# A new hand-written order of TensorE's 531 tasks in an attention and expert-attention kernel

## The chip, the cores and the metric

The kernel runs on one core of a Trainium2 chip. The metric is the time of one execution on the device in microseconds (us), as a median over runs: 588.84 us for the kernel before, over three runs from 587.78 to 590.09.

## What is computed

The inputs are q, k, v of 8 batches, 8 heads, 576 positions and 64 features in float32, a gate matrix and four experts' projections. A first attention with a mask by blocks of 64 runs on every head:

```python
scores = scale * np.matmul(q, k.transpose(0, 1, 3, 2))
mask = block_i >= block_j
attn = softmax(np.where(mask, scores, -1e9))
x = (attn @ v) as (batch, 576, 512)
```

Its output x goes into a mixture of four experts. Each is a causal attention of its own with 64 features (q = x @ wq[e], and so on), followed by a projection to 512. A gate (logits = x @ w_gate) picks two experts for each position, and their outputs are summed with softmax weights.

## The kernel before, in words

Five engines work from in-order queues: TensorE (PE) multiplies, VectorE (DVE) and ScalarE (ACT) do the masks, exponentials and copies, GpSimd (POOL) takes subtractions, SyncE (SP) issues transfers. The program is written out by a planner that runs while the kernel is built. Functions add tasks to `Plan` (line 407), each with an engine, a cost in ns, a key, the tasks that it depends on and the buffers that it takes and frees. `Plan.run` (line 442) then walks through time as the costs have it and gives each engine its next task.

For ACT, DVE, POOL and SP the next task is the one with the lowest key whose buffers are free; `at` (line 339) adds to a key what the table `MOVE` (line 57) holds under the task's name. For PE the order is given: `LINE` (line 311) lists all 531 PE tasks by their number in the order of adding, and PE takes them one by one (lines 456 and 457). PE's planned costs, among them `PRICE` (line 352) for going from one kind of task to another, only set the plan's clock, and so what the other engines choose.

The work is cut into 48 slots: 32 for the first attention (A, batch b, pair of heads p, written here A b.p) and 16 for the experts (M b.p, two pairs of experts for each batch). The PE tasks have four kinds (`mode`):

- S, scores (`f_s`, line 911): q and k in float32 or as a sum of high and low parts (`hl`, `lo`), 64 rows of the array for each head of the pair, so two products run side by side. A slot has three: the one of 448 columns (tiles 0 and 1, named :0), of 448 (tile 2, :2) and of 576 (tile 3, :3). The first slot has four.
- T, transposes (`f_t`, line 978): the exponentials e against a unit matrix, 64 rows each, three for each slot.
- C, attention times values (`f_av`, line 1102): eTa or eTb against va, vm or vz, 128 rows and 64 columns, two for each slot (:0 with eTa, 24 matmuls; :1 with eTb, 32).
- F, full array: projections to the experts' q and k (8 for each batch, 12 matmuls), to v (5), and the output (4 or 5 for each batch, 10 for the last).

Three ways to divide the array follow (`TILING`): S and T use halves of the rows, C halves of the columns, F the whole.

After an S task DVE masks the scores and finds each row's bound (`f_m`), ACT takes the exponentials and their sums (`f_e`), and T can run; DVE or ACT copy the transposes out of PSUM (`f_v`), and C can run. The sums go through ACT and DVE (`f_r1` to `f_rt`), then by a transfer to memory (dr<-rT) and by another back, spread over the partitions (rs<-dr). DVE multiplies the product of a C task with rs (`f_p1`, x<-bank,rs) and so frees its PSUM bank. There are eight banks; `MOST` (line 346) allows at most three of them to C tasks and projections ("m"), two to outputs ("o"), six to scores, six to transposes.

Of the kernel before, what the change touches and what calls it, by code (L numbers as in the profile page):

```python
# [20 lines left out]
P = 128  # L21
# [317 lines left out]
def at(key, b, *tag):  # L339
# [9 lines left out]
FEW = 4  # L349

TILING = {"F": "F", "C": "C", "S": "H", "T": "H"}
PRICE = {"FC": 120, "FS": 197, "FT": 100, "CF": 215, "CS": 182, "CT": 143, "SF": 214, "SC": 155, "ST": 20,
         "TF": 204, "TC": 125, "TS": 33}

STAY = 3.99
# [287 lines left out]
def attention_moe(ctx: ExitStack, tc, qk, v, w, wo, out):  # L643
# [13 lines left out]
    plan = Plan(pools, tc, log)  # L657
# [218 lines left out]
    def add_attention(si):  # L876
        kind, b, p = slots[si]
        causal = kind == "M"
        v_s = V[slots[si]]
        if kind == "A":  # L880
            obuf, odeps = loads[b, p]
            ops = lambda: raw[obuf.idx]
            hl = parts[b, p]
# [534 lines left out]
```

## Time and profile before

| what | value |
| --- | --- |
| median of 3 runs | 588.84 us (587.78 to 590.09) |
| the profiled execution, its own time | 585.91 us |
| span of its trace, first to last instruction | 584.0 us |
| mean granted clock of TensorE in it | 0.998 |

The profiled execution is 2.93 us, or 0.5%, under the median; 1.91 us of its time lie outside the span. Times in the rows below count from the start of the span. In the trace all of the program's instructions carry one line, so they are told apart by tiles: bank<-raw, bank<-hl,lo and their like are S, bank<-id,e is T, bank<-eTa,va (vm, vz) and bank<-eTb,va are C, bank<-x,wh, bank<-wh,x and bank<-woh,y are F.

### The profile page before, as it was taken

The numbers are of one execution on the slowest core, as the hardware profiler recorded it, in microseconds if no ns is written. First come the engines' busy times: TensorE is split into PE (matmuls) and PEld (weight loads), VectorE is DVE, ScalarE is ACT, GpSimd is POOL, SyncE is SP. The second block draws the span as 40 slices with busy tenths as digits, with TensorE's granted clock in tenths as the row PEclk, the third lists the DMA queues.
The fourth block names the chain that finished last, engine by engine and source line by source line (L and its number), as shares of the span: only waits on it lengthen the run. The fifth ranks groups of instructions, "written<-read, shape, count | busy, mean of one in ns | idle before, by whom it ended". The sixth has DMA issues, their size and how long they took to land.

```text
span 584.0 us, 19808 instructions
## 1 busy us (share of the span) xinstructions
PE 567.0 (97%) x7794; PEld 524.8 (90%) x7794; DVE 472.9 (81%) x1669; ACT 449.0 (77%) x1406; POOL 169.5 (29%) x248
## 2 busy tenths in 40 slices
PE   7889999999999999999999999999999999999996
PEld 5779999999999998999999999888999999999874
DVE  7888889799878789988988788898879869964751
ACT  6988789778877778877888688877688869865652
POOL 1275235233331233430425213432221323130101
PEclk9999999999999999999999999999999999999999
DMA  6657134422533225441354212452342403220032
GB/s 229 182 186 236 54 125 112 140 85 67 156 126 92 92 86 167 131 144 42 97 188 145 85 62 85 141 164 83 125 134 85 132 17 97 66 63 21 37 117 90
DMA packets 29852, 65.50 MB, mean 112 GB/s; under 512 B 9664, under 2 KB 10176, under 8 KB 29760
## 3 DMA queue, kind: packets, MB, share of 16 engines
q1 hardware_dynamic: 29616, 64.08, 34.8%
q8 instruction: 61, 1.00, 0.7%
q14 instruction: 31, 0.25, 0.1%
q10 hardware_dynamic: 144, 0.16, 0.1%
HBM read 54.01 MB, written 10.22 MB: 110 GB/s over the span
## 4 chain that ended last, share of the span: by engine, by line
PE 83%; DMA 6%; ACT 4%; DVE 4%; issue 1%; SPq 1%; POOL 0%; DVEq 0%; ACTq 0%
PE bank L389 83%; ACT e L389 2%; DVE bank L389 2%; DMA raw<-in_qk_dram 2%; DMA rs<-dr 2%; DMA out_dram<-ob 1%; DMA dr<-rT 1%; DVE x L389 1%; SPq L389 1%; ACT ob L389 0%; ACT eTb L389 0%; ACT el L389 0%; DVE eTa L389 0%; DVE nm L389 0%; ACT vz L389 0%
## 5 line engine op out<-in xcount | busy, mean ns | idle before, releaser
L389 ACT ACTIVATE e<-bank,nm 128x320 f32<-128x320 f32 (+3 forms) x384 | 218.9, 580 | 24.9 <-DVE nm L389 22.5
L389 DVE CUSTOM_DVE_ANT_0 bank<-bank,mask_a 64x64 f32<-64x64 f32 (+2 forms) x320 | 154.7, 503 | 13.8 <-PE bank L389 6.9
L389 PE MATMUL bank<-x,wh 128*128 128x256 f32 (+1 forms) x512 | 105.0, 299 | 0.0
L389 POOL TENSOR_TENSOR lo<-raw,hl 128x320 fp32r<-128x320 f32 x81 | 68.7, 876 | 114.9 <-ACT hl L389 88.1
L389 PEld LDWEIGHTS bank<-id,e 64*128 64x128 f32 x2112 | 82.1, 139 | 17.3 <-issue 4.7
L389 PE MATMUL bank<-id,e 64*128 64x64 f32 x2112 | 92.0, 226 | 3.3 <-ACT e L389 1.5
L389 PEld LDWEIGHTS bank<-x,wh 128*128 128x128 f32 x512 | 81.9, 188 | 3.3 <-issue 1.5
L389 DVE CUSTOM_DVE_ANT_0 bank<-bank,mask_c 64x64 f32<-64x64 f32 (+4 forms) x160 | 77.4, 505 | 6.1 <-PE bank L389 2.5
L389 ACT ACTIVATION_READ_ACCUMULATOR e<-bank,nm 128x1 f32 x384 | 78.2, 204 | 0.0
L389 PE MATMUL bank<-hl,lo 64*128 64x320 f32 (+2 forms) x352 | 74.8, 380 | 1.6 <-DVE x L389 1.2
L389 PE MATMUL bank<-x,wl 128*128 128x320 f32 (+1 forms) x256 | 75.5, 295 | 0.0
L389 DVE COPY eTb<-bank 128x512 f32<-128x512 f32 (+1 forms) x92 | 58.9, 658 | 15.3 <-PE bank L389 15.0
L389 DVE DVE_READ_ACCUMULATOR2_ANT nm<- 128x1 f32 (+1 forms) x480 | 66.7, 139 | 0.0
L389 PE MATMUL bank<-eTb,va 128*64 128x128 f32 (+2 forms) x1024 | 62.4, 275 | 0.3 <-DVE x L389 0.3
L389 PE MATMUL bank<-hl 64*128 64x320 f32 (+2 forms) x352 | 62.6, 313 | 0.0
L389 PE MATMUL bank<-lo,hl 64*128 64x320 f32 (+2 forms) x352 | 62.4, 312 | 0.0
L389 PEld LDWEIGHTS bank<-eTb,va 128*64 128x64 f32 x1024 | 59.4, 137 | 1.6 <-DVE x L389 0.4
L389 ACT COPY eTb<-bank 128x512 f32<-128x512 f32 (+1 forms) x100 | 52.5, 554 | 9.4 <-PE bank L389 8.7
L389 PE MATMUL bank<-wh,x 128*128 128x260 f32 x288 | 58.6, 287 | 0.0
L389 DVE TENSOR_TENSOR x<-bank,rs 128x256 f32<-128x256 f32 (+1 forms) x144 | 45.6, 349 | 14.3 <-PE bank L389 7.8
L389 POOL TENSOR_TENSOR x<-x,x 128x320 fp32r<-128x320 f32 (+1 forms) x41 | 33.5, 819 | 65.6 <-ACT x L389 45.6
L389 POOL TENSOR_TENSOR lo<-mops,hl 128x288 fp32r<-128x288 f32 (+1 forms) x39 | 28.3, 743 | 83.0 <-ACT hl L389 60.2
(111 smaller groups left out, 1152.6 us busy)
## 6 DMA issues: line engine op xcount, KB each, us to landing
va<-in_v_dram SPq DMA_DIRECT2D x32, 576.0 KB
raw<-in_qk_dram SPq DMA_DIRECT2D x31, 576.0 KB
rs<-dr SPq DMA_DIRECT2D x96, 144.0 KB
out_dram<-ob SPq DMA_DIRECT2D x32, 256.0 KB
raw<-in_w_dram SPq DMA_DIRECT2D x4, 386.0 KB
out_dram<-ob SPq DMA_DIRECT2D x8, 128.0 KB
dr<-rT SPq DMA_DIRECT2D x48, 16.0 KB
raw<-in_wo_dram SPq DMA_DIRECT2D x1, 512.0 KB
```

The source lines that it names most:

```text
L389: r = f(*args, **kwargs)
```

## The change: another order, other keys, other planned prices

The list of tasks, what each computes, its buffers and its dependencies stay. Four things differ: the permutation `LINE`, of which 93 of the 531 places keep their task and a task stands 4.6 places from where it stood on average; the numbers in `MOVE` for tasks of ACT, DVE, POOL and SP; the planned prices `PRICE`; and two planned costs of PE tasks.

```diff
 MOVE = {
-    "0:D0": -14.02, "0:D1": -21.06, "0:D2": 9.4, "0:D3": 28.25, "0:H02": -2.67, "0:H04": 11.73, "0:H12": -14.96,
+    "0:D0": -9, "0:D1": -11.18, "0:D2": 5.22, "0:D3": 26.41, "0:H02": -0.72, "0:H04": 7.01, "0:H12": -0.41,
...
 LINE = [
-    0, 1, 2, 3, 12, 4, 11, 5, 7, 6, 10, 9, 18, 15, 8, 20, 13, 19, 14, 28, 21, 17, 22, 27, 26, 24, 16, 35, 23, 31,
-    30, 29, 25, 34, 33, 32, 36, 44, 43, 38, 53, 58, 50, 52, 37, 42, 51, 57, 60, 46, 63, 39, 54, 47, 73, 65, 64, 62,
...
+    0, 2, 1, 3, 12, 4, 11, 5, 7, 6, 10, 9, 18, 15, 8, 20, 13, 28, 19, 14, 21, 17, 26, 23, 27, 22, 16, 24, 31, 35,
+    29, 30, 25, 34, 33, 32, 44, 37, 36, 43, 38, 52, 53, 50, 39, 42, 51, 56, 62, 46, 64, 65, 45, 60, 58, 54, 47, 63,
...
-PRICE = {"FC": 120, "FS": 197, "FT": 100, "CF": 215, "CS": 182, "CT": 143, "SF": 214, "SC": 155, "ST": 20,
-         "TF": 204, "TC": 125, "TS": 33}
+PRICE = {"FC": 100, "FS": 160, "FT": 80, "CF": 205, "CS": 192, "CT": 145, "SF": 222, "SC": 153, "ST": 0,
+         "TF": 208, "TC": 145, "TS": 18}
...
-            c_s += 193 * last + 25 + (14 if ts_[0] == 0 else 32) + 40 * (hl is None)
+            c_s += 174 * last + 25 + (32 if ts_[0] == 0 else 18) + 40 * (hl is None)
...
-            prev = plan.add("P", (576, 1024)[ch] * 4 / 2.4 + (72, 60)[ch], f_av, at(kk, b, "c", kind, p, ch),
+            prev = plan.add("P", (576, 1024)[ch] * 4 / 2.4 + (60, 62)[ch], f_av, at(kk, b, "c", kind, p, ch),
```

Numbering the tasks in the order of adding and reading both lists gives the kinds of neighbours on PE. How often a task of one kind follows another, over the whole list:

| from, to | before | after |
| --- | --- | --- |
| C to S or T | 37 | 32 |
| S or T to C | 36 | 34 |
| S or T to F | 43 | 41 |
| F to S or T | 42 | 43 |
| F to C | 2 | 0 |
| C to F | 1 | 2 |
| changes of the array's division, sum | 161 | 152 |
| S to T | 32 | 36 |
| T to S | 62 | 75 |

Runs of four C tasks in a row are six before and six after; longer ones are one before (of five) and three after (two of five, and one of six: A4.2:1, M3.0:1, A4.2:0, A4.3:0, A4.3:1, M3.0:0). Between the last S task of a slot and its first C task stand 13 places before and 15 after for slot A5.3, 10 and 9 for A6.1, 16 and 10 for A3.1.

## Rows read from the trace of the kernel before

**Rows 1.** The page: busy time and share of the span by engine.

```profile
PE 567.0 (97%) x7794; PEld 524.8 (90%) x7794; DVE 472.9 (81%) x1669; ACT 449.0 (77%) x1406; POOL 169.5 (29%) x248
```

**Rows 2.** Busy time in stretches: PE, PEld, DVE, ACT, POOL, then clock, DMA share, GB/s.

```profile
0.00:40.00 40.00, 32.03 (x432) 25.82 (x432) 31.78 (x123) 32.67 (x104) 13.45 (x24) 1.00 0.65 211
40.00:556.00 516.00, 513.72 (x7136) 482.16 (x7132) 431.00 (x1516) 405.49 (x1277) 154.25 (x221) 1.00 0.34 105
374.00:383.00 9.00, 7.45 (x132) 6.93 (x127) 6.97 (x27) 6.43 (x20) 3.86 (x6) 1.00 0.44 133
556.00:584.00 28.00, 21.24 (x235) 16.80 (x233) 10.10 (x33) 10.89 (x27) 1.76 (x3) 0.96 0.32 108
```

**Rows 3.** PE's timeline: a C task among C tasks, one after S, one before T.

```profile
79.61 1.22 PE L389 MATMUL bank<-eTa,va 128*64 128x64 f32 x24
80.61 1.94 PE L389 MATMUL bank<-eTb,va 128*64 128x256 f32 x31
...
90.38 0.34 PE L389 MATMUL bank<-eTa,vz 128*64 128x64 f32 x4
...
91.43 0.50 PE L389 MATMUL bank<-eTa,va 128*64 128x64 f32 x6
...
451.36 0.32 PE L389 MATMUL bank<-eTa,vz 128*64 128x64 f32 x4
...
452.51 0.27 PE L389 MATMUL bank<-id,e 64*128 64x64 f32 x2
```

**Rows 4.** The same: an F task among F tasks, one before T, one between S and C.

```profile
107.97 0.41 PE L389 MATMUL bank<-x,wh 128*128 128x256 f32 x2
...
109.41 0.27 PE L389 MATMUL bank<-x,wh 128*128 128x256 f32 x1
...
279.92 0.40 PE L389 MATMUL bank<-x,wh 128*128 128x256 f32 x2
...
281.44 0.28 PE L389 MATMUL bank<-id,e 64*128 64x64 f32 x2
...
225.70 0.51 PE L389 MATMUL bank<-x,wh 128*128 128x256 f32 x2
...
227.32 0.43 PE L389 MATMUL bank<-eTb,vm 128*64 128x256 f32 x2
```

**Rows 5.** The same: S tasks of 576 before S and C, of 448 after S and C.

```profile
249.62 0.41 PE L389 MATMUL bank<-hl,lo 64*128 64x320 f32 x2
...
250.66 0.45 PE L389 MATMUL bank<-hl,lo 64*128 64x448 f32 x2
...
42.05 0.41 PE L389 MATMUL bank<-hl,lo 64*128 64x320 f32 x2
...
43.20 0.43 PE L389 MATMUL bank<-eTb,va 128*64 128x256 f32 x2
...
183.29 0.37 PE L389 MATMUL bank<-hl,lo 64*128 64x448 f32 x2
...
183.90 0.53 PE L389 MATMUL bank<-id,e 64*128 64x64 f32 x12
...
230.26 0.47 PE L389 MATMUL bank<-hl,lo 64*128 64x448 f32 x2
...
230.97 0.41 PE L389 MATMUL bank<-id,e 64*128 64x64 f32 x8
```

**Rows 6.** The chain of waits near 375 us, and the instructions that waited there.

```profile
369.95 3.89 DMA dr<-rT
...
374.41 4.41 DMA rs<-dr
...
378.94 1.02 DVE L389 TENSOR_TENSOR x<-bank,rs 128x256 f32<-128x256 f32 x3 [1.81 <-DMA rs<-dr]
...
380.02 0.41 PE L389 MATMUL bank<-hl,lo 64*128 64x320 f32 x2 [1.22 <-DVE x L389]
```

**Rows 7.** Who waited for whom: us in total, times, longest us.

```profile
PE bank L389 <- ACT ob L389: 1.8, 2, 1.1
```

521 rows, old and new, of tables (LINE, MOVE) are left out of this document.

## The prediction

> **What bounds the kernel now.** I read the page's busy times first, then the table by stretches, then PE's own timeline, and last the chain of waits and the list of who waited for whom. The page shows PE at 567.0 of 584.0 us [rows 1]; DVE and ACT are at 81% and 77%, much, but with room. So it is PE's queue that sets the time, and only two things can shorten it: less idle time, and less time inside what the profile calls busy. The stretches show where the idle time lies [rows 2]. From 40 to 556 us, PE is idle for 516.00 - 513.72 = 2.28 us, and 9.00 - 7.45 = 1.55 us of that lie in one place, from 374 to 383. The first 40 us hold 8.0 us of idle time, in which the first loads and the first exponentials are waited for, and the last 28 us hold 6.8, most of it after PE's last matmul. The granted clock is 1.00, its higher level of 2.4 GHz, in all stretches but the last, which has 0.96. It stayed at 1.00 through the 1.22 us for which PE waited at 380.02 [rows 2, 6].
>
> A busy PE is not a PE that streams all the time. Where one task gives way to a task of another kind, the starts of the tasks stand further apart than inside a run of one kind, and no idle time shows it. This is what an order of the same tasks can change in the middle.
>
> **The change, part by part.** *What goes and comes.* No matmul, copy or transfer is added or taken away. The two lists give 152 changes of the array's division where there were 161, and 17 more steps between S and T (4 from S to T, 13 from T to S), which keep it.
>
> *The price of a change* has two parts, what leaving adds to the task before it and what entering adds to the task behind it; I take both from starts of equal tasks. C: a task of 24 matmuls among its like lasts 80.61 - 79.61 = 1.00 us, behind S 91.43 - 90.38 = 1.05, ahead of T 452.51 - 451.36 = 1.15 [rows 3]. So entering C costs 0.05, leaving it 0.15. F: 12 matmuls among their like last 1.44 us, ahead of T 1.52, between S and C 1.62 [rows 4]: leaving costs 0.08 and, if that also holds towards C, entering 0.10. S: the task of 576 columns lasts 1.04 us ahead of S and 1.15 ahead of C (both behind C), so leaving costs 0.11; the one of 448 lasts 0.61 behind S and 0.71 behind C (both ahead of T), so entering costs 0.10 [rows 5]. T is bounded by S, with which it shares the division.
>
> Sums, leaving plus entering, times the difference of counts: C to S or T 0.25 x -5 = -1.25; S or T to C 0.16 x -2 = -0.32; S or T to F 0.21 x -2 = -0.42; F to S or T 0.18 x +1 = +0.18; F to C 0.13 x -2 = -0.26; C to F 0.25 x +1 = +0.25. Together -1.82 us. The 17 further steps between S and T have no clean pair of rows here. I bound them by 0 (the division stays) and by 0.05, the smallest of the entries above, and take 0.02, nearer to the first since the division stays: +0.3. That gives -1.5 us. If only the leaving counted, the six terms would be -0.75, -0.22, -0.22, +0.08, -0.16 and +0.15, -1.1 in all, and with 17 x 0.05 = 0.85 the gain would be 0.3; if each of the nine had the highest price, 0.25, it would be 2.3.
>
> The Trainium skill says in TensorEngine Tiling (Array Packing), Key Properties, that changing the tiling mode drains TensorE. By that rule alone every change would have one price and the steps between S and T none: nine times the mean of the six prices above, 0.20, is 1.8 us. The rows show unequal prices, higher out of C than out of F, and so the weighted sum stands.
>
> *Idle time in the middle.* The 1.55 us near 380 come from the way of the sums: 3.89 us out to memory, 4.41 us back, then DVE's x, for which PE's S task waited 1.22 us because banks were still held [rows 6]. Four C tasks of three slots had run just before. In the new order slot A5.3 has 15 places between its last S and its first C instead of 13, and its two C tasks run in a run of three; this gap may go. But A6.1 and A3.1 get 9 and 10 places instead of 10 and 16, and runs of five and six C tasks appear, so a gap of the same size can open there. I set these against each other: 0, within -2.3 (all middle idle time gone) and +1.55 for each such place.
>
> *Head and tail.* The first 17 PE tasks keep their order but for a swap of the first two score tasks, which the same first half of the first load feeds; there the loads and ACT set the pace, as before. At the end the last five outputs go through the same two `ob` buffers. Both are taken at 0. At the tail, a copy into `ob` that waits for an earlier transfer held PE for 1.8 us in all [rows 7]; the new order puts batch 6's four output tasks side by side, which does not relieve it.
>
> *The other queues.* New keys and planned costs reorder ACT, DVE, POOL and SP. Each instruction stays, so the sum of their work does too; at 81% and 77% [rows 1] what is late by a task or two is covered by PE's work so long as banks are free. SP's loads and the transfers of the sums are in the same queue and can be shifted against each other: a round of 8.3 us [rows 6] that starts late is what would show. The edits of `PRICE` and of the two planned costs act only through these orders. All of this I cost at 0, with the bounds of the paragraph on idle time.
>
> Sum: -1.5 us. Against the profiled execution that is 585.91 - 1.5 = 584.4; against the median of the runs, from which I count, 588.84 - 1.5 = 587.3.
>
> **The rivals.** *Waits go too.* If the new order also frees the middle of its idle time (-2.3) and the tail of its waits for `ob` (-1.8), 588.84 - 1.5 - 4.1 = 583.2. For it: the gaps are few, and the worst loses its cause. Against it: four outputs side by side, longer runs of C.
>
> *Runs of C that hold the banks.* Slower than before. C tasks and the projections have three banks among them, and a bank comes free only after DVE's x, which needs the sums back. In the run of six, from slots A4.2, A4.3 and M3.0, the fourth C task needs the bank of the first. If sums come late there, PE stands as near 380 us: 1.55 us a place. The first such place eats the gain; from the second on the kernel is slower. At the three runs of five and six, 588.84 - 1.5 + 4.65 = 592.0. For it: the rounds of 8.3 us, and three long runs instead of one. Against it: the one run of five before, and five of its runs of four, share the 2.28 - 1.55 = 0.73 us that PE idles elsewhere in the middle [rows 2].
>
> *Nothing moves.* If entering and leaving costs are hidden or made up by the extra S and T steps (the bound of 0.3 above, or a little more), 588.8.
>
> **How the numbers follow.** The forecast, 587.3, has 0.50; waits go too, 0.28; runs of C, 0.10; nothing moves, 0.12. A measurement of this kernel tells about 0.5%, 2.9 us, from no change, so faster means under 585.9 and slower over 591.8. The forecast's bounds, 0.3 to 2.3 us of gain, with the runs' spread of 1.1 us about their median, reach from 585.5 to 589.6. So faster takes nearly all of the second case and a tenth of the first: 0.27 + 0.06 = 0.33. Slower takes most of the third, 0.08. The rest, 0.59, is the same. The range, 583.2 to 590.1, goes down to the second case and up to no change with the spread of the runs; the case of slower and the lower end of the second stay out, under 2 in 10.
>
> **What would show it.** Right: PE's busy time near 565.5 with 7794 matmuls as before, the same durations of equal tasks between equal neighbours, idle time from 40 to 556 us still about 2 us. The place near 380 us would be without its gap, and others of under 1.5 us in runs of C with x waiting for rs<-dr. Wrong: idle PE time of over 5 us in the middle (the runs of C), a granted clock under 1.00 there, or a gain over 4 us with idle time below 1 us. If busy time does not fall, the prices were read wrongly.

## The result, and the profile after

The changed kernel takes 592.59 us (median of 15 runs, 589.58 to 597.27), the kernel before in the same number of runs 588.84 (585.90 to 593.02). The ratio is 1.0081, with a 95% interval from 1.0058 to 1.0105: 0.8% slower; that is 3.75 us between the medians and 4.8 us by the ratio. The forecast was 587.3 us, and the range ended at 590.1.

The profiled execution of the changed kernel took 595.04 us, 2.45 over its median; that of before lay 2.93 under its own. The two traces thus stand 9.1 us apart where the runs stand 3.75 apart. They show where time goes, and the runs show how much of it is usual.

The page's busy times of the changed kernel (span 593.3 us), to be held against [rows 1]:

```profile
PE 569.8 (96%) x7794; PEld 528.3 (89%) x7794; DVE 484.7 (82%) x1691; ACT 445.6 (75%) x1394; POOL 162.4 (27%) x238
```

The same number of matmuls, 2.8 us more of PE's busy time, and 11.8 us more on DVE, which took over instructions from ACT (-3.4 us) and POOL (-7.1). The table by stretches, with the columns of [rows 2]:

```profile
0.00:40.00 40.00, 31.25 (x413) 25.27 (x414) 32.12 (x117) 32.34 (x103) 13.45 (x25) 1.00 0.67 206
40.00:556.00 516.00, 508.93 (x7087) 478.20 (x7083) 436.09 (x1518) 396.43 (x1247) 148.98 (x214) 1.00 0.33 105
374.00:383.00 9.00, 9.00 (x124) 8.06 (x121) 8.32 (x34) 6.50 (x24) 1.92 (x4) 1.00 0.72 251
556.00:594.00 38.00, 29.59 (x305) 24.85 (x303) 16.52 (x57) 16.84 (x45) 0.00 (x0) 0.94 0.24 81
```

PE's idle time in the middle is 7.07 us, where it was 2.28 [rows 2]. Head and tail add 0.78 and 0.95 us (40.00 - 31.25 against 7.97, and 593.3 - 556 - 29.59 against 6.76). With 2.8 of busy time that makes up the 9.3 us between the spans. The gap of before from 374 to 383 is gone: PE is busy for 9.00 of 9.00 us. Others have come.

The list of whom PE waited for (total us, times, longest us); before, the line on `ob` read 1.8, 2, 1.1 [rows 7]:

```profile
PE bank L388 <- ACT e L388: 4.5, 8, 0.9
PE bank L388 <- ACT ob L388: 2.8, 3, 1.9
PE bank L388 <- DVE eTb L388: 2.5, 2, 1.7
PE bank L388 <- DVE x L388: 2.1, 4, 1.0
PE bank L388 <- ACT eTa L388: 1.9, 1, 1.9
```

Three long waits are new: one of 1.7 us for a DVE copy eTb, one of 1.9 for an ACT copy eTa, one of 1.9 for an output copy `ob`. None of them names a transfer. The timelines of PE, ACT and DVE at these three places do (near 165, 308 and 571 us; in brackets the idle time before the instruction and what ended it):

```profile
165.20 0.30 ACT L388 ACTIVATE r<-ssum,eps 128x10 f32<-128x10 f32 x1 [2.54 <-DMA rs<-dr]
165.53 0.22 DVE L388 RECIPROCAL r<-r 128x10 f32<-128x10 f32 x1 [2.86 <-ACT r L388]
166.71 0.47 PE L388 MATMUL bank<-hl,lo 64*128 64x448 f32 x2 [1.73 <-DVE eTb L388]
...
307.05 0.30 ACT L388 ACTIVATE r<-ssum,eps 128x10 f32<-128x10 f32 x1 [2.07 <-DMA rs<-dr]
308.09 1.03 ACT L388 COPY eTa<-bank 128x448 f32<-128x448 f32 x2
308.69 0.42 PE L388 MATMUL bank<-hl,lo 64*128 64x320 f32 x2 [1.92 <-ACT eTa L388]
...
570.79 0.58 ACT L388 COPY ob<-bank 128x512 f32<-128x512 f32 x1 [2.35 <-DMA out_dram<-ob]
571.43 1.88 PE L388 MATMUL bank<-id,e 64*128 64x64 f32 x37 [1.92 <-ACT ob L388]
```

In each group the first instruction stands at the head of an in-order queue and waits for a buffer that a transfer holds. The first step of a slot's sums, `f_r1` (r<-ssum,eps), needs one of two `r` buffers, and one comes free only when an earlier slot's rs<-dr has landed. Behind it ACT and DVE hold the copies of transposes (eTb, eTa) that free PE's banks. At 571 it is an `ob` buffer that an output still occupies. The chain of waits from 298 us on shows the transfers' own length:

```profile
298.99 4.06 DMA dr<-rT
...
303.61 3.35 DMA rs<-dr
...
307.05 0.30 ACT r L388
307.35 0.85 ACT eTb L388 x2
308.20 0.44 ACT eTa L388
...
308.69 3.40 PE bank L388 x24
```

The granted clock adds to this. Two of these gaps are followed by a stretch at the lower level; the windows (columns as above) around 308 and 571 us:

```profile
305.00:309.00 4.00, 2.08 (x38) 1.82 (x36) 2.27 (x8) 1.95 (x5) 0.00 (x0) 1.00 0.51 178
309.00:313.00 4.00, 4.00 (x40) 3.88 (x38) 3.25 (x14) 3.55 (x16) 0.00 (x0) 0.57 0.22 78
313.00:320.00 7.00, 7.00 (x151) 6.93 (x147) 3.14 (x10) 2.59 (x8) 2.71 (x5) 1.00 0.43 132
...
566.00:572.00 6.00, 3.51 (x55) 2.70 (x56) 3.00 (x12) 2.13 (x7) 0.00 (x0) 1.00 0.40 141
572.00:576.00 4.00, 4.00 (x56) 3.88 (x53) 2.07 (x3) 1.78 (x4) 0.00 (x0) 0.57 0.63 210
```

PE is busy all the time from 309 to 313, but with 40 matmuls in 4 us, against 151 in the 7 us behind (not all of the same size). The 0.57 is the mean of the window; from 310 to 312 the trace has 0.50, the lower level of 1.2 GHz. By estimate a granted clock of 0.57 over 4 us costs 4 x 0.43 = 1.7 us, and the page books it as busy time. Two such stretches, 3.4 us, are more than the 2.8 by which busy time rose.

### The profile page after: what moved, and what is told of

Read it like the earlier page. It is cut to its first block, busy times and chain, and to the rows that moved or that the text cites. A ratio compares the mean times of both kernels' runs of the same rounds, so it can differ in the third digit from the quotient of the medians.

```text
span 593.3 us, 19805 instructions
## 1 busy us (share of the span) xinstructions
PE 569.8 (96%) x7794; PEld 528.3 (89%) x7794; DVE 484.7 (82%) x1691; ACT 445.6 (75%) x1394; POOL 162.4 (27%) x238
## 4 chain that ended last, share of the span: by engine, by line
PE 77%; DMA 10%; DVE 7%; ACT 4%; issue 1%; SPq 1%; DVEq 0%; ACTq 0%
PE bank L388 77%; DMA rs<-dr 3%; DVE bank L388 3%; DMA raw<-in_qk_dram 2%; DMA out_dram<-ob 2%; ACT e L388 2%; DMA dr<-rT 2%; DMA va<-in_v_dram 1%; DVE eTb L388 1%; SPq L388 1%; DVE x L388 1%; ACT ob L388 1%; DVE nm L388 1%; DVE eTa L388 0%; ACT eTb L388 0%
## 5 line engine op out<-in xcount | busy, mean ns | idle before, releaser
L388 DVE CUSTOM_DVE_ANT_0 bank<-bank,mask_a 64x64 f32<-64x64 f32 (+3 forms) x320 | 154.6, 504 | 12.8 <-PE bank L388 6.5
L388 PEld LDWEIGHTS bank<-id,e 64*128 64x128 f32 x2112 | 84.2, 140 | 21.6 <-ACT e L388 8.8
L388 PE MATMUL bank<-id,e 64*128 64x64 f32 x2112 | 94.8, 228 | 7.6 <-ACT e L388 3.2
L388 POOL TENSOR_TENSOR lo<-raw,hl 128x320 fp32r<-128x320 f32 x75 | 64.2, 882 | 102.8 <-ACT hl L388 85.7
L388 DVE CUSTOM_DVE_ANT_0 bank<-bank,mask_c 128x576 f32<-128x576 f32 (+4 forms) x160 | 77.4, 506 | 7.2 <-PE bank L388 3.0
L388 PE MATMUL bank<-hl,lo 64*128 64x320 f32 (+2 forms) x352 | 78.0, 383 | 4.1 <-ACT eTa L388 1.9
L388 DVE COPY eTb<-bank 128x512 f32<-128x512 f32 (+1 forms) x89 | 57.4, 658 | 11.3 <-PE bank L388 10.6
L388 PE MATMUL bank<-hl 64*128 64x320 f32 (+2 forms) x352 | 65.4, 314 | 0.0
L388 PE MATMUL bank<-lo,hl 64*128 64x320 f32 (+2 forms) x352 | 65.1, 314 | 0.0
L388 ACT COPY eTb<-bank 128x512 f32<-128x512 f32 (+1 forms) x103 | 54.7, 552 | 10.4 <-PE bank L388 9.7
L388 DVE TENSOR_TENSOR x<-bank,rs 128x256 f32<-128x256 f32 (+1 forms) x144 | 45.4, 350 | 16.2 <-PE bank L388 11.8
```

Of the source, the lines that this page charges most:

```text
L388: r = f(*args, **kwargs)
```

## The experiments

Each kernel was run in five rounds beside the kernel before. "Orders written out" means that every engine's sequence of tasks was listed as the plan of that kernel had it, so that a buffer more or less doesn't make the planner choose another order.

**More buffers for the sums, in the changed kernel.**

```diff
-                 ... rs=3, r=2, ..., ob=2, nm=60, el=2)
+                 ... rs=3, r=4, ..., ob=2, nm=40, el=2)
```

The pool `nm`, which holds the rows' bounds, gets 40 places instead of 60 in the same edit.

> The changed kernel with every engine's order written out as its plan has it, and four buffers for the sums' reciprocals (r, rT, dr) instead of two, so that ACT's next r no longer waits for an earlier rs<-dr to land. Theory transfers (the new order lost its gain where in-order ACT and DVE stand behind a landing: sums and outputs): the PE gaps near 164 us (2.1 us) and 306 us (2.2 us and what follows) go, 2 to 4 us, so 1.003 times the kernel before. Theory scores (exponentials come late because S and T alternate more; the landings are only the last of several late things): the gaps stay under another name, 1.008.

588.78 us, ratio 1.0023 (1.0002 to 1.0044), as the transfers' theory had it. The same `f_r1` as at 307.05 above has no wait, and PE neither idles nor slows down there:

```profile
305.98 0.31 ACT L396 ACTIVATE r<-ssum,eps 128x10 f32<-128x10 f32 x1
```

```profile
303.00:309.00 6.00, 6.00 (x109) 5.36 (x109) 5.60 (x19) 5.15 (x15) 0.29 (x1) 1.00 0.46 149
309.00:313.00 4.00, 4.00 (x76) 4.00 (x76) 3.50 (x14) 3.96 (x16) 0.21 (x1) 1.00 0.27 85
```

(the first fence is ACT's timeline, the second the windows.) So the gap comes from the two `r` buffers, and the low clock behind it went with the gap. Near 165 us PE waits no longer either (busy for 15.00 us from 155 to 170). Not all is won: over the 12 runs the granted clock is no higher than before this edit (median 0.993 in both), and PE's waits for x<-bank,rs, 2.1 us in all above, are now its longest:

```profile
PE bank L396 <- DVE x L396: 5.2, 6, 2.5
```

The longest of them, 2.45 us, lies in the head, at 34.12 us. This execution of 592.48 us is the slowest of the 12.

**More places for the last outputs, in the changed kernel.** Every second output of batches 6 and 7 leaves through a `raw` buffer, which is idle by then.

```diff
-            ob = Buf("ob", 1)
+            ob = Buf("raw" if b >= 6 and u % 2 else "ob", 1)
+            tiles_ = raw if ob.pool == "raw" else ob_
```

> The changed kernel, orders written out, and every second output of batches 6 and 7 goes through the raw buffers, idle by then, so that a copy into ob no longer waits for the transfer two outputs earlier. Theory transfers: the PE gaps at batch 6's four outputs side by side (0.7 us at 566 and 2.2 us at 569) go, 2 to 3 us, 1.004 times the kernel before. Theory scores: no gain over 0.5 us there, 1.008.

591.07 us, ratio 1.0043 (1.0022 to 1.0064). No wait for `ob` is left in PE's list, and the tail is shorter. The gap near 306 stays, and the low clock too, as the windows show:

```profile
303.00:308.00 5.00, 3.70 (x86) 3.35 (x85) 3.48 (x11) 3.11 (x9) 0.00 (x0) 1.00 0.51 168
308.00:312.00 4.00, 3.56 (x31) 3.44 (x33) 3.45 (x16) 3.39 (x13) 0.00 (x0) 0.60 0.24 80
```

**Both edits, and the sums read early, in both kernels.** The third edit lets rs come from a tensor that is there from the start, so that x waits for no round through memory; an `r` buffer comes free as soon as its dr is written.

```diff
-            rs, dr = rs_[rsb.idx], dr_[rb.idx]
+            rs, src = rs_[rsb.idx], v[0, 0]
...
-        t_ = plan.add("S", 560, f_rw, n_, deps=(t_,), lat=1600)
-        rd = plan.add("S", 1100, f_rd, n_, deps=(t_,), get=(rsb,), rel=(rb,), lat=3200)
+        t_ = plan.add("S", 560, f_rw, n_, deps=(t_,), rel=(rb,), lat=1600)
+        rd = plan.add("S", 1100, f_rd, n_, get=(rsb,), lat=3200)
```

Changed kernel:

> The changed kernel, orders written out, with four r buffers, the outputs' further buffers, and rs read from v (values that have nothing to do with the sums) without waiting for dr to be written, at the same place in SP's queue: some 4 us of each round of the sums are gone. The output is not scaled by the sums. Theory transfers: PE's idle time from 40 to 556 us falls from 7.1 to about 3, and the kernel comes to 0.996 to 1.000 times the one before. Theory scores: idle time stays over 5, 1.004 or more.

Kernel before:

> The kernel before with the same three edits (orders written out as its own plan has them, four r buffers, further buffers for outputs, rs read early from v); the output is not scaled by the sums. Theory transfers: it loses its own gaps near 158 and 380 us and at 561 us, 3 us, to 0.994 to 0.997 times the kernel before, and the changed order with the same edits stands 1 to 2 us under it or level, since the 9 fewer changes of the array's division then show. Theory scores: the changed order with these edits stays 2 us or more over it.

583.48 us (ratio 0.9926, 0.9899 to 0.9953) and 580.55 us (0.9869, 0.9843 to 0.9895). Both orders gain more than was expected, and the new one is still the slower, by 2.9 us: that is what the theory of late scores had expected. But the trace of the changed one has one long gap left, and it stands behind a transfer, the load of the va tile of slot A7.2 (7.14 us in the chain, from 508.28; below PE's timeline and the windows):

```profile
515.55 0.87 PE L396 MATMUL bank<-eTa,va 128*64 128x64 f32 x6 [1.90 <-DMA va<-in_v_dram]
```

```profile
510.00:515.00 5.00, 3.65 (x64) 3.37 (x61) 4.83 (x17) 4.39 (x15) 0.46 (x2) 1.00 0.76 194
515.00:519.00 4.00, 3.44 (x37) 3.48 (x39) 1.36 (x8) 1.30 (x6) 0.00 (x0) 0.57 0.04 11
```

Its 11 runs part by the clock: those at 0.997 or more took 580.8 to 581.7 us, about 1 us over the old order, those at 0.994 or less 583.5 to 586.7. The expectation took the waits behind transfers for those of the sums and outputs alone; the loads can be in it too, which the pair with short loads below tries.

**The two buffer edits alone, in both kernels.**

Kernel before:

> The kernel before, its orders written out, with four r buffers and the outputs' further buffers (raw, for every second output of batches 6 and 7). Theory transfers: it loses its gap near 158 us (0.7 us) and the one at 561 us (1.35 us), 1 to 2 us: 0.9965 to 0.998 times the kernel before, and by that it is the fastest of the kernels that compute everything. Theory scores: 0.999 to 1.001.

Changed kernel:

> The changed kernel with the same two edits. If what they gave one by one (from 1.0081 to 1.0023 and to 1.0043) adds up, 0.9985 times the kernel before; if the stretches of low clock behind the other gaps (the head, 94 and 510 us) stay, 0.998 to 1.001. Theory transfers: level with the kernel before or just under it, and still over the same edits made there. Theory scores: 1.002 or more.

583.86 us (ratio 0.9947, 0.9923 to 0.9972) and 587.39 us (0.9992, 0.9973 to 1.0011). The kernel before with more buffers computes all that it computed, and is the fastest that does: by the ratios 3.1 us under the kernel before, more than was expected, and 7.9 us under the changed one.

**Short loads besides, in both kernels.** The loads of q, k and v from batch 1 on carry 16 of 128 rows (`n_` and `m_` are 16 there).

```diff
-                nc.sync.dma_start(raw[rw.idx], qk[b, p])
+                nc.sync.dma_start(raw[rw.idx][:n_], qk[b, p, :n_])
...
-            nc.sync.dma_start(va[vb.idx], v[b, p])
+            nc.sync.dma_start(va[vb.idx][:m_], v[b, p, :m_])
```

Changed kernel:

> As the changed kernel with all three edits (0.9926), and the loads of v and of q and k from batch 1 on carry 16 of 128 rows, so that they land sooner; scores and values of the other rows are those of earlier tiles, and the output is not scaled by the sums. Theory transfers: the gap near 512 us, behind a load of v, and the low clock after it go; granted clock 0.999 or 1.000 in every run and 2 to 3 us less than before this edit: 0.986 to 0.989. Theory scores: 0.990 to 0.993, gaps remain under the name of ACT's or DVE's scores.

Kernel before:

> The kernel before with all three edits and the same short loads. It had hardly a gap behind a load from batch 1 on, so both theories expect about what it had without this edit, 0.985 to 0.988. Theory transfers: the changed order now stands 0.5 to 2 us under this one or level with it, the price of 9 changes of the array's division. Theory scores: the changed order stays 2 us or more over it.

579.82 us (ratio 0.9864, 0.9843 to 0.9885) and 580.39 us (0.9873, 0.9853 to 0.9893), with a granted clock of 0.999 or 1.000 in all but one of the 12 runs (0.996). Now the new order is level with the old, 0.6 us ahead by the medians, which the intervals don't tell from nothing. The middle of the changed one (windows):

```profile
40.00:556.00 516.00, 514.90 (x7152) 483.56 (x7149) 443.48 (x1547) 403.37 (x1270) 148.67 (x214) 1.00 0.18 51
```

Idle time is down from 7.07 to 1.10 us.

**Short loads alone, in both kernels**, with buffers and sums as they were.

Changed kernel:

> The changed kernel with one edit, the loads of v and of q and k from batch 1 on carry 16 of 128 rows, so that other transfers have the queues nearly to themselves; buffers, the sums' way and all orders stay. If the loads make the sums and outputs late, as they did the va tile at 512 us: the waits near 164, 306 and 568 us shrink with the durations of rs<-dr and of the outputs, idle time from 40 to 556 us is under 3 us, and 584 us or less, ratio under 0.993. Rival, the two r and two ob buffers bind whatever the loads do: the waits near 306 and 568 us stay, with the low clock behind them, 589 to 592 us, ratio 1.001 to 1.006.

Kernel before:

> The kernel before with the same one edit. If the old order has few waits that the loads cause: 586 to 588 us, ratio 0.995 to 1.000. If its waits come from the loads too, 584 us or less, as the changed one, ratio under 0.993.

587.40 us (ratio 0.9995, 0.9972 to 1.0019) and 584.99 us (0.9953, 0.9931 to 0.9974). The first time lies between its two expectations, the second ratio at the lower end of its first. The trace of the changed one is of its fastest execution, 584.06 us, 3.3 under the median. In it PE's idle time from 40 to 556 us is 1.00 us, and the `f_r1` of the same slot finds its buffer free, though there are two as before (ACT's timeline):

```profile
299.98 0.31 ACT L388 ACTIVATE r<-ssum,eps 128x10 f32<-128x10 f32 x1
```

The tail's waits for `ob` stay, 2.3 us in all. So in this execution two `r` buffers are enough once the loads are short: it is beside the full loads that the sums' transfers land too late for them. The median run, with a clock of 0.991 to 0.998 over the 12, is not explained by this trace.

**Only the price of changes.** On top of the last kernel before, twenty neighbouring pairs in PE's order are exchanged (14 of S with F, 6 of C with S), which makes 201 changes of the array's division out of 161. The unexchanged kernel ran beside it once more.

> The kernel before with its three edits for landings and the short loads of v and of q and k (x7_before_all_short, 580.39 us), and in PE's written-out order twenty neighbouring pairs of tasks exchanged, 6 of them C with S and 14 S with F; this adds 40 changes of the array's division (14 pairs F to S and back, 6 pairs C to S and back) and alters neither a task nor a buffer. The prediction's prices hold as sums: 14 x (0.18 + 0.21) + 6 x (0.25 + 0.16) = 7.9 us more, so 588.3 us, 1.000 to 1.001 of the kernel before. Rival, the changes lie beside waits of PE that are there anyway: 0 to 2 us more, 580.4 to 582.4, ratio 0.987 to 0.990. Second rival, the exchanges make scores late as well: more than 8 us, over 1.002, with PE idle time up by what is beyond 8.

> x7_before_all_short once more, as the neighbour of p1_swaps on the same chip: 580.4 us, ratio 0.987.

596.51 us (ratio 1.0137, 1.0116 to 1.0157) against 581.22 (0.9878, 0.9859 to 0.9898): 15.3 us more, so the second rival. The pages and the middle windows, first of the unexchanged kernel, then of the exchanged one:

```profile
PE 566.1 (98%) x7794; PEld 524.6 (91%) x7794; DVE 472.9 (82%) x1671; ACT 449.3 (78%) x1406; POOL 169.5 (29%) x248
```

```profile
40.00:556.00 516.00, 515.32 (x7165) 483.64 (x7162) 433.32 (x1524) 407.91 (x1283) 154.49 (x222) 1.00 0.17 51
```

```profile
PE 576.1 (97%) x7794; PEld 525.4 (88%) x7794; DVE 474.6 (80%) x1671; ACT 448.0 (75%) x1406; POOL 169.5 (29%) x248
```

```profile
40.00:556.00 516.00, 508.64 (x7021) 470.68 (x7018) 421.94 (x1475) 393.67 (x1240) 152.35 (x218) 1.00 0.17 50
```

At the same clock and with the same matmuls, PE's busy time rises by 10.0 us, 0.25 for each added change, where the prediction's prices gave 7.9. The other 5.5 us are idle time (spans of 594.7 and 579.2), and PE's wait for e has doubled from 2.9 to 5.9 us in all, which fits the second rival's reason, that a score issued one task later delays its exponentials.

## Why the prediction was wrong

**The table of pairs.** With the same edits in both kernels, the difference of the two ratios times 588 us is what the new order costs:

| edits in both kernels | changed | before | the order's cost, us |
| --- | --- | --- | --- |
| none | 1.0081 | 1 | +4.8 |
| more buffers | 0.9992 | 0.9947 | +2.6 |
| short loads | 0.9995 | 0.9953 | +2.5 |
| more buffers, sums read early | 0.9926 | 0.9869 | +3.4 |
| all three, and short loads | 0.9864 | 0.9873 | -0.5 |

Each difference is certain to about 2 us, so the three middle rows can't be told apart; the first and the last can. By their middle values buffers alone or loads alone take away about half; with all three edits and the short loads, nothing of the loss is left that the runs could tell. So the loss is in waits behind transfers, with the low clock that follows some of them, and the two orders are worth about the same without them.

**The price of changes** was the one gain in the sum, -1.5 us, and no run shows it. Equal tasks between equal neighbours do last as long as before: an F task of 12 matmuls among its like 1.44 us [rows 4], a C task behind S 1.05 [rows 3] (PE's timeline of the changed kernel; the first two rows are the starts of an F task and of the next one):

```profile
53.48 0.41 PE L388 MATMUL bank<-x,wh 128*128 128x256 f32 x2
...
54.92 0.45 PE L388 MATMUL bank<-x,wh 128*128 128x320 f32 x2
...
91.60 1.24 PE L388 MATMUL bank<-eTa,va 128*64 128x64 f32 x24
92.65 0.31 PE L388 MATMUL bank<-eTa,vz 128*64 128x64 f32 x4
```

The price exists, too: the exchanged pairs cost 0.25 us of busy time for each added change, where the prediction's prices gave 0.20. The Trainium skill's rule (TensorEngine Tiling (Array Packing), Key Properties) that a change of tiling mode drains TensorE fits this. But nine changes fewer did not shorten PE's busy time. In the changed kernel it rose by 2.8 us, and without the 3.4 us that are put down to the clock it would have fallen by 0.6. The pair with all three edits and short loads, both with the middle at a clock of 1.00, has the same busy time in the new order (first line) and in the old (second line; 566.1 when it ran again):

```profile
PE 566.5 (98%) x7794; PEld 524.7 (91%) x7794; DVE 484.6 (84%) x1693; ACT 445.4 (77%) x1394; POOL 162.5 (28%) x238
...
PE 566.5 (98%) x7794; PEld 524.3 (91%) x7794; DVE 472.8 (82%) x1671; ACT 448.6 (78%) x1406; POOL 169.5 (29%) x248
```

The prediction had named this sign itself: "If busy time does not fall, the prices were read wrongly." Where the 1.5 us went stays open. One hint: prices fitted to the starts of PE's tasks from 41 to 556 us (a duration for each form, a price for each pair of kinds, without tasks that waited or ran at low clock) give, as an estimate, 1.8 to 2.0 us less for the new order in six traces of the old one, but only 0.6 to 0.7 in seven traces of the new. A price read beside one order's neighbours did not hold beside the other's.

**The step that failed** is the term for idle time in the middle, "I set these against each other: 0". In the profiled execution the middle's idle time rose by 4.79 us, and with it came low clock; four `r` buffers alone took the changed kernel from 1.0081 to 1.0023. The step saw the landing of rs<-dr only through DVE's x and the banks of C tasks [rows 6]; that gap went, as the step thought it might. It did not ask which other instructions wait for the same landing. ACT's `f_r1` does, for its buffer, and what stands behind it on ACT and DVE are the copies that PE needs. The trace of before has that wait once, 1.0 us long, in the list of ACT's waits, and its chain of waits leads from a landing through it to ACT's copy; the prediction uses neither:

```profile
ACT r L389 <- DMA rs<-dr: 1.0, 1, 1.0
...
152.94 5.03 DMA rs<-dr
...
158.07 0.30 ACT r L389
158.38 0.86 ACT eTb L389 x2
```

After, it stands twice and 2.5 us long:

```profile
ACT r L388 <- DMA rs<-dr: 4.6, 2, 2.5
```

**The other queues** were costed at 0, on the ground that what is late by a task or two is covered. A wait of 2.5 us at the head of ACT's queue is not covered. "The sum of their work" stayed nearly, +1.3 us over the three engines, but not its split (DVE +11.8 us); whether this costs time was not tried apart.

**Head and tail** were taken at 0. Four outputs side by side don't relieve the two `ob` buffers, I wrote, and stopped there; in the new order PE waits for them longer, 2.8 us instead of 1.8, and a second stretch at the lower clock follows. (ACT's own waits for a free `ob` are no longer, 5.7 us against 6.2; what stands behind them differs.) The edit of the outputs takes 0.4% off the changed kernel. The cause of the head's 0.78 us stays open.

**The rivals.** *Runs of C that hold the banks* named 592.0 us, but not the place: of four waits for x, 2.1 us in all, the longest is 1.0, and the run of six C tasks behind 308 us is slow by its clock. Nor does it come out where the `r` buffers no longer bind: of the 5.2 us of waits for x with four of them, 2.45 lie in the head, and near the run of six only 0.47 and 0.35 (at 315 and 320 us). So its number was near the result (592.59) by luck. Its chance was put at 0.10, with the ground that the long runs of before idled so little, which says nothing of an order in which the transfers fall elsewhere. *Nothing moves* was right on one point: the order of the tasks by itself gained nothing that shows. As for signs, "over 5 us in the middle" and "a granted clock under 1.00 there" were named as the wrong outcome, and both came (7.07 us, and 0.57 from 309 to 313).

**The clock's part.** Over the 15 runs of the changed kernel the time rises by 0.66 us for each 0.001 of mean granted clock that is lost. Its median clock is 0.993; 28 runs of the kernel before, taken beside the first experiments, had 0.995. So some 1.3 us of the loss are clock, as far as this goes.

**What stays open.** Why `f_r1` meets an rs<-dr that has not landed at 164 and 306 us was not traced to single keys, and no run has the new `LINE` with the old keys and prices, or the other way round, so which part of the change brings the waits is not shown. The plan lets the sums' read-back land after 3.2 us, and the chains of the changed kernel show 3.35 to 5.89; that the new order rests on the plan's shorter time was not tried.

## What to carry to other kernels

Ask of each landing that the critical engine waits for who else waits for it: for its data, but also for the buffer that it frees. An instruction that waits for a buffer at the head of an in-order queue passes its wait on to everything behind it, so before trusting a new order, read the waits of the helpers on DMA as well as those of the bound engine. Check a price that was read from a few rows by its sum, here PE's busy time, beside equal edits. And with little slack in the buffers, look there before the order: two more `r` buffers and a spare place for outputs made the kernel before 0.5% faster, where the new order made it 0.8% slower.

## What was not expected of the hardware

Waits of PE of under 2 us were followed by a fall of the granted clock: after 1.92 us at 308.69 and 1.92 at 571.43 it was 0.57 over the next 4 us, and after 1.90 at 515.55 in the kernel with three edits likewise. Length alone does not part the cases: with places for the last outputs, a wait of 1.75 at 308.44 was followed by 0.60 over 4 us, while the one of 1.73 that ended at 166.71 was followed by nothing of the kind, and neither was the one of 1.22 us in the kernel before [rows 6].

The same small transfer takes quite different times. In the changed kernel rs<-dr took 5.89 us from 159.20 on, with the DMA engines busy to 0.92 from 160 to 167, and 3.35 us from 303.61 on, with 0.51 from 305 to 309. That company sets its time is not shown: in the kernel before it took 4.41 us with 0.44 [rows 2, 6].
